# Woven rows: the order in device memory of the keys and values of a decode step on one core

## The chip, the cores and the metric

The kernel runs on one core of one Trainium2 chip. The metric is device microseconds (us) from launch to end. Three executions of the kernel before took 1299.92, 1299.98 and 1300.0 us; their median is 1299.98 us. The profile is of one more execution, of 1300.05 us, whose span from the first to the last instruction is 1298.7 us.

## The reference

One new token for each of two sequences (B = 2) attends to a cache of 32,768 positions. There are 32 query heads of 128 elements, and 8 heads of keys and values; each group of four query heads shares one of them. A small dense branch with a squared ReLU gates the result. Everything is float32.

```python
xn = layernorm(x)                                   # (2, 1, 512)
q = xn @ wq                                         # 32 heads of 128
scores = einsum("bhqd,bhkd->bhqk", q, k) * 128**-0.5
o = einsum("bhqk,bhkd->bhqd", softmax(scores), v)   # k, v: (2, 8, 32768, 128), each used by 4 heads
s = o.reshape(2, 1, 4096) @ wo
h = relu(xn @ w1 + b1); g = silu((h * h) @ w2 + b2)
out = x + s * g
```

Keys and values are 2 x 8 x 32768 x 128 x 4 bytes each, 268 MB, and each element is used once, for four heads. That is 537 of the 561 MB that the kernel reads.

## The kernel before, in words

**Tiles.** The 16 pairs of a sequence and a head of keys are taken one after the other, each in two halves of 16,384 positions: 32 half heads. For each there is one tile of keys and one of values. A tile is 128 partitions of 16,384 float32, that is 128 rows of 64 KiB, 8 MiB in all. For keys a partition is one of the 128 elements of a head, and its row runs over the positions; for values a partition is one position of each 128, and its row holds 128 positions with their 128 elements.

**Buffers.** There is one buffer for keys (kslot), one for values (vslot) and one for weights (wbuf), each of 64 KiB in every partition. A tile is not held twice: the next tile of keys may be fetched when the scores of the present one have been computed, and the next tile of values when the sums over the present one are done.

**Order of the work.** TensorE (PE) computes the scores of half head i from kslot (L351, 32 products of 512 columns, the queries being the stationary side), then the transposes that the softmax needs (L354, L357, L359), then the sums over the values from vslot (L368), then turns the result (L378). VectorE (DVE) and ScalarE (ACT) do the maximum, the exponential and the merging of the two halves. All of it runs in loops over the 32 half heads, written by hand with semaphores, one loop for each engine.

**The queue of fetches.** SyncE (SP) issues nearly all transfers, in the order of the program: first the weights of the dense branch (wm, into vslot) and wq (into wbuf), then the first tile of keys (L121). When the prologue has used vslot, the first tile of values follows (L231). Then, for each half head, SP waits for the scores (L240) and issues the next tile of keys (L241), waits for the sums over the values (L242) and issues the next tile of values (L244). The last tile of values comes in two halves by columns (L246, L247). After that follow the pieces of the output weights wo (L330). Each transfer is one instruction. The 16 DMA engines carry out a transfer together, each a share of its rows, and each takes up the next transfer in the queue when it is done with its share of the last.

**Rows in device memory.** In the host arrays `kt` and `vt` the row of partition p is row p of its tile, and after each row of 64 KiB lies a gap of GAP = 256 unused floats (1 KiB), put there by `gapped`. A fetch names 128 rows with a step of 16,640 floats at the source and 128 partitions at the destination. The weights wm, wq and wo lie without gaps.

Of the kernel before, what the change touches and what calls it, by code (L numbers as in the profile page):

```python
# [14 lines left out]
P = 128  # L15
B, D, HQ, HKV, SK, DH, F = 2, 512, 32, 8, 32768, 128, 1792
REP = HQ // HKV
NS = B * HKV
ND = D // P
NG = 4  # L20
# [4 lines left out]
SLOT = HALF  # L25
# [7 lines left out]
TAIL = (2, 1, 1)  # L33
NX = PIECES[0]
LINE = 256
GAP = 256
SCALE = 1.0 / math.sqrt(DH)


# [18 lines left out]
def build(nc, xr, x16, kt, vt, wq, wm, wo, out):  # L58
# [4 lines left out]

    def sb(name, *shape):
        return nc.alloc_sbuf_tensor(name, [P, *shape], F32)

    nc.sbuf_base = -(-nc.sbuf_base // LINE) * LINE
    kslot, vslot, wbuf = sb("kslot", SLOT), sb("vslot", SLOT), sb("wbuf", SLOT)
    prob, pT, o_sb = sb("prob", W), sb("pT", W), sb("o_sb", W)
    oS, oX, oN = sb("oS", NS, REP), sb("oX", NX, 16), sb("oN", TOP, M)  # L70
    ident = sb("ident", P)
    xb, gate, yb, gpad = sb("xb", P), sb("gate", P), sb("yb", P), sb("gpad", P)
# [11 lines left out]
    gv, ge, gb, gc, gd, gs, dm, ex, os, vh = (nc.alloc_semaphore(n) for n in ("gv", "ge", "gb", "gc", "gd", "gs", "dm", "ex", "os", "vh"))  # L84
# [17 lines left out]
    g, v = nc.gpsimd, nc.vector  # L102
# [15 lines left out]
    t_pad = pool.done(g.memset(vslot[:, WM:], 0.0))  # L118
    sp.wait(t_pad)
    nc.sync.dma_start(wbuf[:, :], wq).then_inc(wq_sem, 16)  # L120
    nc.sync.dma_start(kslot[:, :], kt[0, 0, :, 0:SLOT]).then_inc(gs, 16)  # L121
    nc.regs_mov(ss, 1)
    sp_hint = nc.sync.mark_branch_hint_location()
    v.memset(o_ps[:, :], 0.0).then_inc(dm, PRO)
# [49 lines left out]
    def pro(n, i):  # L174
        return pe.sem, 2 * i + n
# [52 lines left out]
    dve.wait(t_qz, t_q)  # L228
    v.tensor_copy(qz[:, 28:32], qT[:, 0, :]).then_inc(gs, 1)
    sp.wait(pro(VD, 2))  # L230
    nc.sync.dma_start(vslot[:, :], vt[0, 0, :, 0:SLOT]).then_inc(gv, 16)  # L231

    SD, MT, PT, LS, VD, OT = range(1, 7)

    def at(n, i):
        return pe.sem, 2 * PRO + 6 * i + n

    for i in range(NT - 1):
        s, u = divmod(i + 1, 2)
        sp.wait(at(SD, i))  # L240
        nc.sync.dma_start(kslot[:, :], kt[s, u, :, 0:SLOT]).then_inc(gs, 16)  # L241
        sp.wait(at(VD, i))  # L242
        if i + 2 < NT:
            nc.sync.dma_start(vslot[:, :], vt[s, u, :, 0:SLOT]).then_inc(gv, 16)  # L244
        else:
            nc.sync.dma_start(vslot[:, 0:SLOT // 2], vt[s, u, :, 0:SLOT // 2]).then_inc(gv, 16)  # L246
            nc.sync.dma_start(vslot[:, SLOT // 2:], vt[s, u, :, SLOT // 2:SLOT]).then_inc(gb, 16)  # L247
    nc.br("sp_last", engines=SP)

    dve.wait(t_selm, t_qT)  # L250
# [193 lines left out]
def packed(A_x, A_k_cache, A_v_cache, A_wq, A_wo, B_w1, B_b1, B_w2, B_b2):  # L444

    def c(a):
        return np.ascontiguousarray(a)

    def gapped(a):
        rows = np.zeros((NS, 2, P, SLOT + GAP), np.float32)  # L450
        rows[..., :SLOT] = a
        return rows

    x = np.asarray(A_x).reshape(B, D)
    k = np.asarray(A_k_cache).transpose(1, 0, 3, 2).reshape(NS, DH, 2, HALF).transpose(0, 2, 1, 3)
    v = np.asarray(A_v_cache).transpose(1, 0, 2, 3).reshape(NS, 2, NG, NJ, 4, P, DH).transpose(0, 1, 5, 4, 2, 3, 6).reshape(NS, 2, P, SLOT)
    wq = np.asarray(A_wq).reshape(ND, P, HQ * DH).transpose(1, 0, 2).reshape(P, SLOT)
    w1 = np.asarray(B_w1).reshape(ND, P, NF, P)
    w2 = np.asarray(B_w2).reshape(NF, P, D)
    wm = np.zeros((28, 4, P, P), np.float32)  # L460
    for d in range(ND):
        wm[4 * d:4 * d + 3] = w1[d][:, :12].reshape(P, 3, 4, P).transpose(1, 2, 0, 3)
        wm[3 + 4 * (d // 2), 2 * (d % 2):2 * (d % 2) + 2] = w1[d][:, 12:].transpose(1, 0, 2)
    wm[[11, 15] + list(range(16, 28))] = w2.reshape(NF, P, 4, P).transpose(0, 2, 1, 3)
    wm = np.concatenate([wm.transpose(2, 0, 1, 3).reshape(P, WM), np.zeros((P, SLOT - WM), np.float32)], axis=1)
    w = np.asarray(A_wo).reshape(HQ, DH, D)
    parts, h = [], 0
    for n in PIECES + TAIL:
        parts.append(w[h:h + n].transpose(1, 0, 2).reshape(n * P, D))
        h += n  # L470
    xr = np.zeros((8, D), np.float32)
    xr[:B] = x
    xr[B:6].reshape(-1)[:F] = np.asarray(B_b1)
    xr[6] = np.asarray(B_b2)
    return {"xr": c(xr.reshape(8, 2, D // 2).transpose(1, 0, 2)), "x16": c(x.reshape(B, NG, P).transpose(1, 0, 2).reshape(NG * B, P)), "kt": gapped(k), "vt": gapped(v), "wq": c(wq),
            "wm": c(wm), "wo": c(np.concatenate(parts))}


# [13 lines left out]
```

## Time and profile before

| | |
|---|---|
| median of three executions | 1299.98 us (1299.92 to 1300.0) |
| profiled execution, its span | 1300.05 us, 1298.7 us |
| PE busy | 689.8 us, 53% of the span |
| ACT, DVE busy | 99.1 us, 85.8 us |
| DMA queue of SP | 10,800 packets, 561.06 MB, 99.8% of 16 engines' span |
| read from device memory | 561.01 MB, 432 GB/s over the span |
| mean granted TensorE clock | 0.752 |

The page of the profile groups instructions by line, engine and tile, with the idle time of the engine before them and what ended it. A row of the chain of waits says when a piece of the work that ended last began, how long it lasted, and what it was; a transfer there is counted from its issue to its landing, with the time in the queue. A window gives, for a stretch of time, the busy time of each engine, the share of the DMA engines' time in which they moved packets, and the rate.

### The profile page before, as it was taken

To read this page: it belongs to the slowest core of one execution; us is meant where nothing else is said; L and a number is where in the kernel's file an instruction comes from. 1 tells how busy PE (TensorE), PEld (TensorE's weight loads), DVE (VectorE), ACT (ScalarE), POOL (GpSimd) and SP (SyncE) were. 2 spreads that over 40 slices of the span, in tenths; PEclk is the share of its full clock that TensorE was granted. 3 is DMA by queue.
4 is the path that set the end of the run, shared out by engine and by line. 5 is a ranking of instruction groups with operands and counts; after the bars stand their busy time and mean duration, and the time that the engine had idled before them with its cause. 6 is when DMAs were issued, how large, how long until landed. Compare 5 with 4: busy or idle time off the path is not lost.

```text
span 1298.7 us, 11201 instructions
## 1 busy us (share of the span) xinstructions
PE 689.8 (53%) x4781; PEld 191.1 (15%) x4781; DVE 85.8 (7%) x366; ACT 99.1 (8%) x202; POOL 5.7 (0%) x22
## 2 busy tenths in 40 slices
PE   3646546545645545544545644554654654554557
PEld 0111111111111111111111111111111111111112
DVE  2100000000000000000000000000000000000001
ACT  0301000010010001001000000001001000100100
POOL 1000000000000000000000000000000000000000
PEclk9877677778678777768777767767767777876878
DMA  9999999999999999999999999999999999999998
GB/s 420 420 452 420 446 426 420 452 420 452 420 452 420 442 430 420 452 420 452 420 452 420 442 430 420 452 420 452 420 452 420 444 428 424 448 420 452 420 436 373
DMA packets 10840, 561.08 MB, mean 432 GB/s; under 512 B 1216, under 2 KB 1368, under 8 KB 1752
## 3 DMA queue, kind: packets, MB, share of 16 engines
q1 hardware_dynamic: 10800, 561.06, 99.8%
q10 hardware_dynamic: 40, 0.02, 0.0%
HBM read 561.01 MB, written 0.07 MB: 432 GB/s over the span
## 4 chain that ended last, share of the span: by engine, by line
DMA 74%; PE 24%; issue 1%; DVE 0%; POOL 0%; SPq 0%; POOLq 0%
DMA vslot<-in_vt 70%; PE o_ps L368 24%; DMA wbuf<-in_wo 3%; DMA vslot<-in_wm 1%; PE wb L396 0%; DVE vslot L210 0%; PE acc L426 0%; PE acc L430 0%; POOL pT L201 0%; POOL pT L183 0%; SPq L247 0%; DVE pT L208 0%; SPq L246 0%; DVE yb L434 0%; DVE xb L436 0%
## 5 line engine op out<-in xcount | busy, mean ns | idle before, releaser
L368 PE MATMUL o_ps<-vslot,pT 128*16 128x512 f32 x2304 | 324.5, 726 | 223.1 <-DMA vslot<-in_vt 199.4
L351 PE MATMUL sc<-kslot,qz 128*32 128x512 f32 x2048 | 294.0, 739 | 279.2 <-DMA kslot<-in_kt 279.2
L351 PEld LDWEIGHTS sc<-kslot,qz 128*32 128x32 f32 x2048 | 71.3, 132 | 480.4 <-DMA kslot<-in_kt 286.8
L368 PEld LDWEIGHTS o_ps<-vslot,pT 128*16 128x16 f32 x2304 | 69.2, 112 | 449.2 <-issue 220.9
L313 ACT ACTIVATE prob<-sc,nm 128x512 f32<-128x512 f32 x32 | 22.0, 687 | 635.8 <-DVE nm L281 635.8
L274 DVE TENSOR_REDUCE r<-sc 128x1 f32<-128x512 f32 x32 | 22.1, 692 | 559.7 <-PE sc L351 559.7
L322 ACT COPY o_sb<-o_ps 128x512 f32<-128x512 f32 x32 | 18.7, 585 | 476.9 <-PE o_ps L368 476.9
L357 PE MATMUL tp<-ident,prob 128*128 128x128 f32 x128 | 26.9, 346 | 50.6 <-ACT prob L313 50.6
L295 DVE TENSOR_REDUCE t<-ot 128x4 f32<-128x64 f32 x32 | 7.2, 224 | 544.7 <-PE ot L378 544.7
L378 PE MATMUL ot<-ident,o_sb 128*128 128x128 f32 x140 | 23.0, 287 | 25.1 <-ACT o_sb L322 22.9
L357 PEld LDWEIGHTS tp<-ident,prob 128*128 128x128 f32 x128 | 17.2, 171 | 56.7 <-ACT prob L313 56.7
L354 PE MATMUL ms<-ident,r 128*128 128x128 f32 x32 | 10.3, 323 | 26.4 <-DVE r L274 26.4
L378 PEld LDWEIGHTS ot<-ident,o_sb 128*128 128x128 f32 x140 | 14.7, 141 | 57.3 <-ACT o_sb L322 52.4
L315 ACT COPY pT<-tp 128x512 f32<-128x512 f32 x32 | 18.7, 585 | 29.8 <-PE tp L357 29.8
L313 ACT ACT_TABLE_LOAD x16 | 20.5, 1283 | 0.3
L359 PEld LDWEIGHTS ms<-selh,l 128*128 128x128 f32 x64 | 12.9, 249 | 0.0
L354 PEld LDWEIGHTS ms<-ident,r 128*128 128x128 f32 x32 | 4.3, 133 | 55.4 <-DVE r L274 55.4
L359 PE MATMUL ms<-selh,l 128*128 128x4 f32 x64 | 10.9, 241 | 0.0
L277 DVE TENSOR_REDUCE mh<-ms 128x4 f32<-128x128 f32 x32 | 9.3, 291 | 10.9 <-PE ms L354 10.9
L204 ACT COPY vslot<-wbuf 128x4096 f32<-128x4096 f32 x2 | 7.1, 3605 | 0.2 <-DMA wbuf<-in_wq 0.2
L313 ACT ACTIVATION_READ_ACCUMULATOR prob<-sc,nm 128x1 f32 x32 | 6.2, 193 | 0.0
L396 PE MATMUL wb<-wbuf,oX 128*16 128x512 f32 x24 | 4.5, 906 | 2.2 <-DMA wbuf<-in_wo 2.2
(86 smaller groups left out, 78.1 us busy)
## 6 DMA issues: line engine op xcount, KB each, us to landing
vslot<-in_vt SPq DMA_DIRECT2D x2, 4096.0 KB, 23.9
vslot<-in_wm SPq DMA_DIRECT2D x1, 7168.0 KB, 19.4
wbuf<-in_wo SPq DMA_DIRECT2D x1, 3072.0 KB, 34.8
vslot<-in_wo SPq DMA_DIRECT2D x1, 2048.0 KB, 13.5
vslot<-in_wo SPq DMA_DIRECT2D x2, 1024.0 KB, 11.9
kslot<-in_kt SPq DMA_DIRECT2D x32, 29.4
wbuf<-in_wo SPq DMA_DIRECT2D x1, 512.0 KB, 13.8
wbuf<-in_wo SPq DMA_DIRECT2D x2, 256.0 KB, 14.0
```

The lines of the kernel that those rows point to most:

```text
L274: v.tensor_reduce(r1[:, :], sc[:, :], axis=AX.X, op=ALU.max).then_inc(dm, 1)
L277: did(f"mh{u}", v.tensor_reduce(mh[:, u, :], ms[:, :P].rearrange("p (a h) -> p h a", h=REP), axis=AX.X, op=ALU.max))
L295: did(f"t4{u}", v.tensor_reduce(t4[:, u, :], ot[:, :].rearrange("p (i y e) -> p e i y", i=4, y=NG)[:, :REP], axis=AX.XY, op=ALU.add))
L313: nc.scalar.activation(prob[:, :], sc[:, :], AF.Exp, bias=nm[:, u:u + 1], scale=SCALE, accum_out=l1[:, :]).then_inc(ex, 1)
L315: copy(pT[:, :], tp[:, :]).then_inc(gv, 1)
L322: copy(o_sb[:, :], o_ps[:, :]).then_inc(os, 1)
L351: ins = mm(sc[32 * c:32 * c + 32, :], qz[:, 28 - 4 * j:60 - 4 * j], kslot[:, lo:lo + W], start=(j == 0), stop=(j == NJ - 1))
L354: tr(ms[:, :P], r1[:, :].to_broadcast([P, P]), ident[:, :]).then_inc(pe.sem, 1)
L357: ins = tr(tp[:, k * P:(k + 1) * P], prob[:, k * P:(k + 1) * P], ident[:, :])
L359: mm(ms[:, :REP], l1[:, :].to_broadcast([P, P]), selh[:, :], start=True, stop=True).then_inc(pe.sem, 1)
L368: ins = mm(o_ps[32 * y:32 * y + 16, :], pT[:, 16 * n:16 * n + 16], vslot[:, n * W:(n + 1) * W], start=(n < NG), stop=(n >= 32 - NG))
L378: ins = tr(ot[:, lo:lo + P], o_sb[:, n * DH:(n + 1) * DH], ident[:, :])
```

## The change

Three things change together, for the tiles of keys and values alone.

- **No gap.** The rows of a tile lie one behind the other, 64 KiB each, and a tile is one block of 8 MiB.
- **The order of the rows.** `woven` puts the row of partition 8e + j at place 16j + e of the tile (e from 0 to 15, j from 0 to 7). So the rows of partitions 0, 8, 16, ... 120 come first, in one stretch of 1 MiB, then those of 1, 9, ... 121, and so on.
- **The form of the fetch.** The new helper `fetch` names the source as 16 times 8 rows: the outer dimension (e, 16 long) has a step of one row, the inner one (j, 8 long) a step of 16 rows. The destination is the same 128 partitions as before, in their order. All six places that fetch keys or values go through it, the two halves of the last tile of values too.

The program has the same instructions in the same order on every engine; the tiles hold the same numbers in the same places as before. The weights are fetched as before.

```diff
-GAP = 256
+NE = 16
...
+    def fetch(dst, src, sem):
+        nc.sync.dma_start(dst, src.rearrange("(j e) c -> e j c", e=NE)).then_inc(sem, 16)
...
-    nc.sync.dma_start(kslot[:, :], kt[0, 0, :, 0:SLOT]).then_inc(gs, 16)
+    fetch(kslot[:, :], kt[0, 0], gs)
...
-    nc.sync.dma_start(vslot[:, :], vt[0, 0, :, 0:SLOT]).then_inc(gv, 16)
+    fetch(vslot[:, :], vt[0, 0], gv)
...
         sp.wait(at(SD, i))
-        nc.sync.dma_start(kslot[:, :], kt[s, u, :, 0:SLOT]).then_inc(gs, 16)
+        fetch(kslot[:, :], kt[s, u], gs)
         sp.wait(at(VD, i))
         if i + 2 < NT:
-            nc.sync.dma_start(vslot[:, :], vt[s, u, :, 0:SLOT]).then_inc(gv, 16)
+            fetch(vslot[:, :], vt[s, u], gv)
         else:
-            nc.sync.dma_start(vslot[:, 0:SLOT // 2], vt[s, u, :, 0:SLOT // 2]).then_inc(gv, 16)
-            nc.sync.dma_start(vslot[:, SLOT // 2:], vt[s, u, :, SLOT // 2:SLOT]).then_inc(gb, 16)
+            fetch(vslot[:, 0:SLOT // 2], vt[s, u][:, 0:SLOT // 2], gv)
+            fetch(vslot[:, SLOT // 2:], vt[s, u][:, SLOT // 2:], gb)
...
-    def gapped(a):
-        rows = np.zeros((NS, 2, P, SLOT + GAP), np.float32)
-        rows[..., :SLOT] = a
-        return rows
+    def woven(a):
+        return np.ascontiguousarray(a.reshape(NS, 2, NE, P // NE, SLOT).transpose(0, 1, 3, 2, 4)).reshape(NS, 2, P, SLOT)
...
-"kt": gapped(k), "vt": gapped(v), "wq": c(wq),
+"kt": woven(k), "vt": woven(v), "wq": c(wq),
```

More of the change, by code (lines that the diff above doesn't have):

```diff
@@ L474, in packed @@
     xr[6] = np.asarray(B_b2)
-    return {"xr": c(xr.reshape(8, 2, D // 2).transpose(1, 0, 2)), "x16": c(x.reshape(B, NG, P).transpose(1, 0, 2).reshape(NG * B, P)), "kt": gapped(k), "vt": gapped(v), "wq": c(wq),
+    return {"xr": c(xr.reshape(8, 2, D // 2).transpose(1, 0, 2)), "x16": c(x.reshape(B, NG, P).transpose(1, 0, 2).reshape(NG * B, P)), "kt": woven(k), "vt": woven(v), "wq": c(wq),
             "wm": c(wm), "wo": c(np.concatenate(parts))}
```

## The prediction

> **What bounds the kernel now.** I read the page first: the DMA rows, the chain of waits, then the two groups in which TensorE does most of its work.
>
> ```profile
> span 1298.7 us, 11201 instructions
> ...
> DMA packets 10840, 561.08 MB, mean 432 GB/s; under 512 B 1216, under 2 KB 1368, under 8 KB 1752
> q1 hardware_dynamic: 10800, 561.06, 99.8%
> ...
> DMA 74%; PE 24%; issue 1%; DVE 0%; POOL 0%; SPq 0%; POOLq 0%
> ...
> L368 PE MATMUL o_ps<-vslot,pT 128*16 128x512 f32 x2304 | 324.5, 726 | 223.1 <-DMA vslot<-in_vt 199.4
> L351 PE MATMUL sc<-kslot,qz 128*32 128x512 f32 x2048 | 294.0, 739 | 279.2 <-DMA kslot<-in_kt 279.2
> ```
>
> The 16 DMA engines move packets for 99.8% of the span, and both large groups of TensorE sit idle for transfers (279.2 and 199.4 us). The 24% of PE in the chain are therefore not a second bound: they stand ahead of an issue, while the queue still works on the other buffer's tile. The chain in order of time (start, length, what) shows the cadence:
>
> ```profile
> 50.36 27.74 DMA vslot<-in_vt
> 78.10 0.04 issue
> 78.14 9.07 PE o_ps L368 x64
> ...
> 281.14 29.02 DMA vslot<-in_vt
> ...
> 319.31 29.44 DMA vslot<-in_vt
> ...
> 1207.36 30.11 DMA vslot<-in_vt
> ...
> 1248.60 34.82 DMA wbuf<-in_wo
> ```
>
> The first tile of values has landed at 78.10, the 31st at 1207.36 + 30.11 = 1237.47. Between them lie 30 tiles of values and 30 of keys: 1159.37 / 60 = **19.32 us a tile**. A tile is 128 rows of 65,536 bytes, so each of 16 engines moves 8 rows, 2.415 us a row, 27.1 GB/s an engine and 434 GB/s in all. All 64 tiles take 64 x 19.32 = 1236 us of the 1298.7; the rest is weights and the two ends.
>
> **What the rate does not depend on.** Three windows: the start of wm, the whole of wq, and the middle of the kernel (the last two columns are the DMA engines' busy share and GB/s).
>
> ```profile
> 1.70:4.50 2.80, 0.00 (x0) 0.00 (x0) 0.89 (x5) 1.28 (x1) 2.80 (x12) 1.00 1.10 369
> 19.40:38.70 19.30, 16.72 (x132) 4.10 (x132) 0.89 (x6) 0.58 (x1) 0.52 (x1) 1.00 1.00 431
> 600.00:1200.00 600.00, 321.21 (x2164) 89.29 (x2168) 34.97 (x157) 41.46 (x94) 0.00 (x0) 0.73 1.00 433
> ```
>
> wq is a tile of the same shape without gaps, and it moves at 431 GB/s, the gapped tiles at 433. Only the first packets of all, just after the launch, are slower (369). Next, three windows of 3 us in 40 slices of 75 ns, in which a packet's bytes stand where it starts: around the first row of keys (38 to 41 us), then 600 to 603 and 1200 to 1203.
>
> ```profile
> GB/s 0 0 0 0 0 0 0 0 874 1748 3495 1748 1748 2622 1748 0 0 0 0 0 0 0 0 0 0 0 0 0 0 0 0 0 0 0 0 0 0 0 0 0
> ```
>
> ```profile
> GB/s 0 0 0 0 0 0 0 0 0 0 0 0 0 0 0 0 0 0 0 0 0 3495 4369 874 874 1748 2621 0 0 0 0 0 0 0 0 0 0 0 0 0
> ```
>
> ```profile
> GB/s 0 0 0 0 0 0 3495 4369 874 874 1748 1748 874 0 0 0 0 0 0 0 0 0 0 0 0 0 0 0 0 0 0 0 0 0 0 0 0 0 2621 4369
> ```
>
> In each, the 16 engines start a row within 6 or 7 slices, some 0.5 us, and then none starts for 1.8 us or more. They are as closely in step after 1200 us as at 39. No engine falls behind, wherever its rows lie. I read from this that what sets 2.415 us a row is fixed in width, one to an engine, and lies behind the reading of device memory: in the engine itself, or where it writes.
>
> **The change part by part.** *No gap, and the rows woven at the source.* This touches the reading, which by the rows above does not set the pace. The bound on a gain: the two landings at 281.14 + 29.02 = 310.16 and 319.31 + 29.44 = 348.75 are 38.59 apart, the shortest two tiles I found, against 38.64 on the mean. Were all 32 pairs as short, 32 x 0.05 = 1.6 us would go, 0.12%. I take 0. The bound on a loss: the 369 GB/s of the first packets throughout, 1236 x (433/369 - 1) = +214 us; wq speaks for the other end, and I take 0 here too.
>
> *The issue of a fetch.* The program has the same 65 fetches. Their instruction has one more dimension. The issue times (least, median, most, in ns) of keys, and the slowest issue in the trace, that of a small input from ACT:
>
> ```profile
> L241 SPq DMA_DIRECT2D kslot<-in_kt x31: 327/328/328, 67.3 to 1227.3; - x31
> DMA to landing us min/median/max: 28.4/29.4/53.3
> ```
>
> ```profile
> L132 ACTq DMA_DIRECT2D xb<-in_x x1: 647/647/647, 2.1 to 2.1; - x1
> ```
>
> From 0.33 us to at most 0.65 is 0.32 more, 65 x 0.32 = 21 us if nothing hid it. It is hidden: a tile lands 29.4 us after its issue and takes 19.32, so it waits 10.1 us behind the other buffer's tile; if tiles get longer, this cover grows. I take 0.
>
> *Which partitions an engine writes.* The source now has an outer dimension of 16 where it had 128 rows. With 16 engines, the natural share of engine e is index e: 8 rows at the source, and at the destination the 8 neighbouring partitions 8e to 8e + 7, in that order. Every large transfer in the trace has 128 rows on both sides, so none shows such a split, nor does the trace tell which partitions an engine writes now. Two ends: if each engine still has what it writes into to itself, a tile stays at 19.32 us and the term is 0. If under the new split the engines meet two by two at one of the places that an engine has had to itself until now, with the others left idle, each gets half: 4.83 us a row, 38.64 us a tile, and 64 x 19.32 = **+1236 us**. Of the two I take the upper end. The rows point to a private path of fixed width as the limit, and the split at the destination is the one thing in this change that can take the privacy away.
>
> [...]
>
> Do the pairs stay in step? The spread of 0.5 us at the first row of keys is at most 0.2 of a row. [...] A tile has landed when its slowest pair has, so the pair closest in step decides, and I take 1.98, +1211 us.
>
> **The sum.** The span of 1298.7, and 1300.05 - 1298.7 = 1.35 around it: 1300.05 + 1211 + 0 + 0 = 2511 us; the profiled execution stands 0.07 us from the median of 1299.98. The queue does not run dry: keys are issued 9 us after their tile has landed (9.07 above for the values' products), while 38 us of the other tile are still to come. The stall goes to TensorE, which waits some 38 us more for each pair of tiles; nothing else is late. I say **2511 us**, 2410 to 2600 for this case (the lower end by 0.4 row of distance within pairs, 1300 + 0.9 x 1236; the upper if a tile takes 2.5% more than twice its time, 39.6 us).
>
> **The rivals.**
>
> *It changes nothing (1300 us, 1298 to 1302).* The split at the destination may be as good as the old one: because the limit sits in the engine and not where it writes, or because the hardware deals out the partitions as before whatever the source says. For it: rows take the same time for every tensor, and an engine of fixed width would look exactly like this. Against it: nothing in the trace, only that the form of the fetch is new. It decides if one row of keys still takes 2.415 us. This is the end on the other side.
>
> [...]
>
> *The sources collide (1300 + 214 = 1514 us).* Sixteen reads 64 KiB apart in step could keep meeting in one part of device memory, as perhaps the first packets do (369 GB/s). Against it: wq, without gaps, at 431.
>
> *Faster.* It would take more than the 1.6 us bounded above.
>
> **How the numbers follow.** In step 0.60, slipping apart 0.15, nothing 0.20, sources 0.03, faster 0.02. About 0.2%, 2.6 us, is what a measurement of this kernel can tell from no change. Slower is 0.60 + 0.15 + 0.03 = 0.78, the same 0.20, faster 0.02. Leaving out the case of no change would leave out more than 2 in 10, so the range reaches from it to the top of the likeliest: 1298 to 2600. It is wide because it holds two outcomes with little between; the likeliest alone is 2410 to 2600.
>
> **What would show it.** Right: the median time to landing of keys goes from 29.4 to about 38.3 - 9.1 + 38.3 = 67 us, the landings of values come some 76 us apart, a window in the middle shows about 219 GB/s with a DMA share still near 1.00, since each packet takes twice as long and no engine rests, and the idle time ahead of L351 grows by some 600 us. Wrong in its mechanism, though slow: a share near 0.5 at the same packet length (fewer engines at work), more packets of a smaller size (rows cut up), or a rate that climbs in the course of the kernel (pairs slipping apart). Wrong altogether: 433 GB/s and 38.6 us between landings, as before.

## The result, and the profile after

The changed kernel takes 2654.11 us (median of six executions, 2649.69 to 2655.28); the kernel before took 1299.93 us beside it. The ratio is 2.041, with a 95% interval of 2.039 to 2.0431. The predicted time was 2511 us and the range 1298 to 2600. The direction was as forecast, and so was the place of the loss, the destination (205 GB/s at partitions 0 to 63 against 413 at 32 to 95, below); the loss, 1354 us, was larger than the 1211 that were predicted.

The page of the changed kernel, at the places that were shown of before:

```profile
span 2653.3 us, 11201 instructions
...
DMA packets 10840, 561.08 MB, mean 211 GB/s; under 512 B 1216, under 2 KB 1368, under 8 KB 1752
...
q1 hardware_dynamic: 10800, 561.06, 100.0%
...
another core or an unknown queue 69%; PE 25%; DVE 2%; DMA 2%; issue 1%; ACT 1%; POOL 0%; SPq 0%; POOLq 0%; DVEq 0%
...
L371 PE MATMUL o_ps<-vslot,pT 128*16 128x512 f32 x2304 | 326.4, 729 | 900.9 <-DMA vslot<-in_vt 877.0
L354 PE MATMUL sc<-kslot,qz 128*32 128x512 f32 x2048 | 294.4, 740 | 956.0 <-DMA kslot<-in_kt 956.0
```

There are as many packets and as many bytes as before, and the engines rest no more than before (100.0% of 16 engines' span). They move half as much in the same time: 211 GB/s instead of 432. TensorE works as long as before (294.4 us against 294.0 in the scores), and its idle time ahead of the scores has grown by 677 us. The chain of waits no longer names the transfers: a transfer now lands 72 us after its issue, and the view puts such a wait down to an unknown queue. The groups still name them.

The windows, with the start (wq, fetched as before) first, then the middle; the last two columns are the DMA share and GB/s:

```profile
19.40:38.70 19.30, 16.39 (x132) 4.05 (x132) 0.89 (x6) 0.98 (x2) 0.89 (x2) 1.00 1.00 431
...
600.00:1200.00 600.00, 151.25 (x1041) 41.20 (x1041) 16.41 (x75) 20.24 (x44) 0.00 (x0) 0.62 1.01 208
```

wq, in the old form, still moves at 431 GB/s. The slow rate begins with the first fetch of the new form. The issues of keys and values, from SP's instructions in order of time (start, length), and the issues of the keys' tile with the times to landing:

```profile
89.59 0.54 SPq L68 DMA_DIRECT2D kslot<-in_kt  x1
130.32 0.54 SPq L68 DMA_DIRECT2D vslot<-in_vt  x1
...
2519.77 0.54 SPq L68 DMA_DIRECT2D kslot<-in_kt  x1
```

```profile
L68 SPq DMA_DIRECT2D kslot<-in_kt x32: 536/537/654, 5.4 to 2519.8; - x32
...
DMA to landing us min/median/max: 70.9/71.7/74.7
```

From the second issue of keys to the last there are 30 pairs of tiles: (2519.77 - 89.59) / 60 = **40.50 us a tile**, against 19.32 before. 64 x (40.50 - 19.32) = 1356 us, which is the whole loss. In the packet records of the trace the rows of keys and values come in fours: one of 4.92 us, then three of 5.12.

### The profile page after: what moved, and what is told of

It is laid out like the page before. It is cut to its first block, busy times and chain, and to the rows that moved or that the text cites. A ratio compares the mean times of both kernels' runs of the same rounds, so it can differ in the third digit from the quotient of the medians.

```text
span 2653.3 us, 11201 instructions
## 1 busy us (share of the span) xinstructions
PE 690.6 (26%) x4781; PEld 190.7 (7%) x4781; DVE 86.1 (3%) x366; ACT 99.1 (4%) x202; POOL 5.7 (0%) x22
## 4 chain that ended last, share of the span: by engine, by line
another core or an unknown queue 69%; PE 25%; DVE 2%; DMA 2%; issue 1%; ACT 1%; POOL 0%; SPq 0%; POOLq 0%; DVEq 0%
PE o_ps L371 11%; PE sc L354 11%; DMA wbuf<-in_wq 1%; PE tp L360 1%; DVE r L277 1%; PE ot L381 1%; ACT o_sb L325 1%; DMA wbuf<-in_wo 0%; PE ms L357 0%; DVE mh L280 0%; ACT prob L316 0%; DVE mm L282 0%; DVE nm L284 0%; PE ms L362 0%
## 5 line engine op out<-in xcount | busy, mean ns | idle before, releaser
L354 PE MATMUL sc<-kslot,qz 128*32 128x512 f32 x2048 | 294.4, 740 | 956.0 <-DMA kslot<-in_kt 956.0
L320 ACT COPY lh<-ms 128x4 f32<-128x4 f32 x32 | 5.4, 168 | 0.0
## 6 DMA issues: line engine op xcount, KB each, us to landing
vslot<-in_wm SPq DMA_DIRECT2D x1, 7168.0 KB, 19.3
kslot<-in_kt SPq DMA_DIRECT2D x32, 71.7
```

What stands on the lines that cost most here:

```text
L354: ins = mm(sc[32 * c:32 * c + 32, :], qz[:, 28 - 4 * j:60 - 4 * j], kslot[:, lo:lo + W], start=(j == 0), stop=(j == NJ - 1))
```

## The experiments

Two theories were at odds with each other, and each could still have taken part. *Where it writes*: by the form of the new fetch an engine writes 8 neighbouring partitions, and the engines meet two by two at places that take one engine's rate. *What it reads, or how it is asked to*: rows without gaps side by side collide when they are read in step, or the longer form of the fetch is slower by itself. And for the size: is the time above twice the old (40.5 instead of 38.6 us) part of the meeting, or something added by the reading? The trace does not name the engine of a packet: which engine writes which partitions, and how many meet at a place, is inferred from the form of the fetch, here and in the expectations. That four neighbouring partitions are one place, and that partitions 32 apart in one half share one, is supposed there and tested by rates alone. The rates and the lengths of the rows are measured.

**No gap, old form.** The kernel before with one number changed.

```diff
-GAP = 256
+GAP = 0
```

> The kernel before with GAP = 0: the rows of a tile lie one behind the other, and the fetch names 128 rows as before. It does one part of the change alone, the missing gap. If the place of the writing decides (the engines meet where they write), the gap is innocent: 1300 us, within 0.2%. [...]

It took 1299.91 us; the ratio is 1.0001, interval 0.9991 to 1.0011. Its window from 600 to 1200 us:

```profile
600.00:1200.00 600.00, 318.49 (x2164) 87.94 (x2168) 35.02 (x157) 41.46 (x94) 0.00 (x0) 0.74 1.00 433
```

The missing gap is innocent, and by itself it brings nothing either.

**New form, rows in the order of the partitions, with gaps.** Nothing is woven here; only the split is that of the change. A ninth row, unused, follows every eight, so that the source keeps its two steps.

```diff
+GAP = 256
...
-        nc.sync.dma_start(dst, src.rearrange("(j e) c -> e j c", e=NE)).then_inc(sem, 16)
+        nc.sync.dma_start(dst, src).then_inc(sem, 16)
...
-    fetch(kslot[:, :], kt[0, 0], gs)
+    fetch(kslot[:, :], kt[0, 0, :, 0:8, 0:SLOT], gs)
...
+        rows = np.zeros((NS, 2, NE, P // NE + 1, SLOT + GAP), np.float32)
+        rows[:, :, :, :P // NE, :SLOT] = a.reshape(NS, 2, NE, P // NE, SLOT)
...
```

> The new form of the fetch (16 times 8 rows) over rows that lie in the order of the partitions, each with its gap of 1 KiB: nothing is woven, no rows lie side by side without a gap. It undoes the source's part of the change and keeps the split. If the place of the writing decides: as the changed kernel, 2654 us within 1%, and the 4.8% above twice the time of a tile (40.5 us instead of 38.6) are there too, since they belong to the sharing. If reading woven rows decides: 1300 us. If the sharing costs exactly half and the woven reading the 4.8% on top: 1300 + 64 x 19.32 = 2536 us less the distance within pairs, so 2510 to 2536.

It took 2652.69 us, a ratio of 2.0405 (2.0365 to 2.0446), and the window reads as that of the changed kernel:

```profile
600.00:1200.00 600.00, 152.76 (x1041) 42.38 (x1041) 16.41 (x75) 20.24 (x44) 0.00 (x0) 0.61 1.00 206
```

So the order of the rows in device memory has no part that shows in the loss, nor in the excess over twice the time. Left are the form and the destination.

**The same fetch at two destinations.** After the first tile of keys, both kernels fetch 64 rows a tile in the new form, from the same woven rows. They differ in one number, the partition at which the 64 rows begin: BASE is 0 in the one shown and 32 in the other.

```diff
+BASE, ROWS = 0, 64
...
-        nc.sync.dma_start(dst, src.rearrange("(j e) c -> e j c", e=NE)).then_inc(sem, 16)
+        nc.sync.dma_start(dst[BASE:BASE + ROWS], src[0:ROWS].rearrange("(j e) c -> e j c", e=NE)).then_inc(sem, 16)
```

> The changed kernel, but after the first tile of keys each fetch brings only 64 rows into partitions 0 to 63 (the other partitions keep what stood there, so half of the keys and values are left out). Each engine gets 4 neighbouring partitions: engine e partitions 4e to 4e+3. If places 32 partitions apart are shared, engines e and e+8 meet all the time: 5.12 us a row, 20.3 us a half tile, 206 GB/s at a DMA share of 1.00, the whole 19 + 63 x 20.3 + 64 = 1360 us. If what counts is the form or the woven source alone: the same as the next run.

> As the run at partition 0 in every word of the fetch, but the 64 rows go to partitions 32 to 95 (the others keep what stood there). Engine e writes partitions 32+4e to 35+4e; if partitions p and p+32 of one half of 64 share a place, no two engines meet. Then a row takes 2.42 us, 27.1 GB/s an engine: rate over DMA share 433 GB/s, a half tile 9.7 us, and TensorE with some 24 us a half head becomes the bound: 800 to 900 us in all. If the form of the fetch or the woven source slows the engines: 206 GB/s at a share of 1.00 and 1360 us, as at partition 0.

At partition 0 it took 1372.8 us, at partition 32 780.13. The windows, first at 0, then at 32:

```profile
300.00:1200.00 900.00, 420.61 (x3058) 114.35 (x3058) 48.97 (x220) 59.57 (x132) 0.00 (x0) 0.75 1.00 205
```

```profile
300.00:700.00 400.00, 320.56 (x2530) 97.15 (x2526) 40.25 (x181) 49.33 (x109) 0.00 (x0) 0.91 0.92 380
```

205 GB/s at a share of 1.00 against 380 / 0.92 = 413. In the packet records the rows at 0 take 5.12 us, the fourth like the first, and the median row at 32 takes 2.42. (Some rows at 32 are longer, up to 4.03 us, mostly where the engines start again after a rest; hence 413 and not 433.) The form, the source and the number of bytes are the same, so the destination alone makes the difference. (At 32 the transfers no longer bound all of it: the chain of waits goes to TensorE for 50% of the span and to transfers for 40%.) This is the experiment that settles what sets the rate. That engine e writes the partitions from 4e on at 0 (from 32 + 4e at 32), and which of them meet, is inferred from the form; that it matters which 64 partitions are written is measured.

**16 and 32 rows at partition 0.** The kernel at partition 0 with `BASE, ROWS = 0, 16` and `0, 32`.

> After the first tile of keys each fetch brings only 16 rows into partitions 0 to 15, one to an engine (seven eighths of the keys and values are left out). Four engines then write four neighbouring partitions. If four neighbours share one place, a row takes four times as long: 9.66 us if sharing itself costs nothing, 10.24 us and 102 GB/s at a DMA share of 1.00 if it costs the 5.9% that two show (5.12 against 4.83), whatever their number; more than 10.4 us and under 101 GB/s if the cost grows with the number. If only places 32 partitions apart were shared, 433 GB/s. TensorE or the chain of a half head becomes the bound, some 24 us each, 800 us in all; the rate is read over the DMA share.

> The same with 32 rows into partitions 0 to 31, two to an engine (three quarters of the keys and values are left out): engines 2i and 2i+1 write the same four neighbouring partitions, and none of them is 32 partitions from another's. If four neighbours share a place: 5.12 us a row, 206 GB/s over the DMA share, as with engines 32 partitions apart, so that the cost of sharing is the same for both ways of meeting. If only the distance of 32 makes them meet: 2.42 us a row and 433 GB/s.

They took 769.54 and 779.41 us. Their windows, 16 rows first:

```profile
200.00:700.00 500.00, 411.31 (x3207) 126.64 (x3211) 50.87 (x230) 63.19 (x142) 0.00 (x0) 0.89 0.84 97
```

```profile
200.00:700.00 500.00, 404.12 (x3137) 121.50 (x3141) 49.92 (x226) 61.59 (x137) 0.00 (x0) 0.89 0.92 191
```

With 32 rows, 191 / 0.92 = 208 GB/s, and 5.12 us at the median row of the packet records: the price of the 64 rows at 0 (205 GB/s, 5.12 us). So at the same rate of 205 to 208, partitions 32 to 63 add nothing to what 0 to 31 take. By the form of the fetch, two engines write the same four neighbours here, and there two write 32 partitions apart. With 16 rows, 97 / 0.84 = 115 GB/s, more than the 102 that I had expected from the price of two. The engines start and stop here, which blurs the rate; in the packet records the rows range from 7.1 to 9.64 us. The tiles come in pairs without a pause between them. In the second of a pair, where I take four engines to be at work at a place from a row's beginning to its end, the rows gather at 9.60 to 9.64 us (136 of the 928 rows after 100 us, none longer). If four share a place there, that is 4 x 65,536 bytes in 9.64 us, **27.2 GB/s** for the place: 9.64 us is less than four times 2.418 (9.67), so the excess of the two is not there.

**Keys in pieces, old form, all the work done.** The kernel before, each tile of keys in fetches of 16, or of 64, partitions in their order, with the gaps. The one by 16 is shown; in the other, 64 stands for 16 and `i * 33 + 1` for `i * 129 + 1`.

```diff
+    def pieces(dst, src, sem):
+        for p in range(0, P, 16):
+            nc.sync.dma_start(dst[p:p + 16], src[p:p + 16]).then_inc(sem, 16)
...
-        nc.sync.dma_start(kslot[:, :], kt[s, u, :, 0:SLOT]).then_inc(gs, 16)
+        pieces(kslot, kt[s, u, :, 0:SLOT], gs)
...
-        w(gs, i * 17 + 1)
+        w(gs, i * 129 + 1)
```

> The kernel before, but each tile of keys comes in eight fetches of 16 partitions in their order, one row for each engine, old form, gaps kept. All the work is done. Four engines share a place, for all of a tile. If sharing costs nothing more than the division: 4 x 2.415 = 9.66 us a row, 77.3 us a tile of keys, 1300 + 32 x 58.0 = 3155 us. If each sharing costs 5.9%, as for two: 10.23 us, 81.8 us a tile, 3300 us. If the cost grows with the number: above 3350 us.

> The kernel before, but each tile of keys comes in two fetches of 64 partitions, old form of the source (64 rows one after the other), gaps kept. All the work is done. Partitions 0 to 63 hold only half of the places, so two engines share each. If the price belongs to two engines at one place, however the fetch is written: 5.12 us a row, 41 us a tile of keys, 1300 + 32 x 21.6 = 1992 us, 1970 to 2000. If the 5.9% belong to the new form or the woven rows: 38.6 us a tile and 1918 us. If only the new form makes engines meet: 1300 us.

By 64 it took 1994.63 us (ratio 1.5345, interval 1.5314 to 1.5375), as expected for two at one place (5.12 us a row), though the form of the source is the old one. By 16, two executions took 3111.41 and 3223.99 us; the profile is of the longer one. A tile of keys in each, the windows reaching from its first row to the first row of the next tile, 16 first:

```profile
132.70:206.00 73.30, 9.28 (x68) 2.27 (x68) 0.23 (x1) 0.59 (x1) 0.00 (x0) 0.57 1.00 114
```

```profile
98.50:138.70 40.20, 10.47 (x68) 2.45 (x68) 0.23 (x1) 0.59 (x1) 0.00 (x0) 0.58 1.01 209
```

By 64, two at one place by the form of the fetch, it is 40.2 us a tile, more than twice 19.32 (38.6). By 16, four at one place, it is 73.3 us, less than four times 19.32 (77.3), but I do not take this for the rate of one place. In the packet records the 16 engines begin the second row of this tile up to 1.7 us apart, and 32 rows at partition 0 moved 208 GB/s where 16 moved 115. From these I infer that an engine that is ahead already writes at the next place while the others are still at the last; no run shows it. For four at one place I go by the run with 16 rows, 9.64 us a row. Neither run shows a tax on every sharing: the excess is there with two (40.2 us against 38.6), and not with four (9.64 us a row against 9.67). Three were not tried.

The expectation of 3155 us for no excess lies between the two times, but not for its reason. With 73.3 us a tile it would be 1300 + 32 x 54.0 = 3028 us. The profiled execution took 196 us more, and most of that is not accounted for. In its later part the values' rows take about 2.75 us instead of 2.42, which adds some 33 us to an engine's time over the whole profile, and single rows among them take 3 to 5 us (packet records). From 2000 to 3000 us the rate is 166 GB/s at a share of 0.95, which is 101 us for a pair of tiles instead of 73.3 + 19.3.

**The change for the keys alone**, with the values in the old form, without their gap and with it; the one without is shown, the other fetches `vt[s, u, :, 0:SLOT]`.

```diff
-            fetch(vslot[:, :], vt[s, u], gv)
+            nc.sync.dma_start(vslot[:, :], vt[s, u]).then_inc(gv, 16)
...
-"kt": woven(k), "vt": woven(v), "wq": c(wq),
+"kt": woven(k), "vt": c(v), "wq": c(wq),
```

> The change for the keys alone; the values are fetched as 128 rows without gap. If each tile is priced by its own split, 32 tiles of keys at 40.5 us and 32 of values at 19.3: 1300 + 32 x 21.16 = 1977 us, 1965 to 1990. If the fetches of keys leave the engines out of step for the values or the other way round: under 1950 us.

> The change for the keys alone as before, but the values keep their gap of 1 KiB. In the run without that gap the values' rows took 2.418 us in some tiles and 2.714 us in others, the same for all 128 rows of a tile. If the missing gap is the cause (rows read in step collide at the source): all tiles of values at 2.418 us, 1977 to 1985 us, with a spread of a few us between executions. If it comes from the change of the split between two tiles: again tiles at 2.714 us, and times from 1980 to 2040 us.

Without the gap, the profiled execution took 1998.87 us, and another 2029.35. Two stretches of it, one in the first tile of values and one in the fourth:

```profile
80.00:99.00 19.00, 9.61 (x71) 2.94 (x71) 1.38 (x5) 1.43 (x4) 0.00 (x0) 0.77 1.00 386
267.00:284.00 17.00, 9.99 (x71) 3.01 (x71) 2.29 (x11) 1.54 (x5) 0.00 (x0) 0.80 1.00 432
```

In the packet records, 25 of the 32 tiles of values take 2.418 us a row and 7 take 2.714. 7 x 8 x 0.296 = 17 us, so 1982 without them: the sum of the two prices holds to 0.3%. With the gap, the median row of every tile of values of the profiled execution takes 2.418 us and it took 1986.93 us, but the four executions scatter: 1986.93, 1987.69, 2026.33 and 2133.55 us. That is neither what the first theory expected (a spread of a few us) nor, in the one that was profiled, the second. In the run by 16 above, the values have their gap, and their rows slow down all the same. So a missing gap is not needed for it. What slows the values' rows between the slow tiles of keys is open; the whole-kernel change does not show it, since there no tile of keys or values is in the old form.

## Why the prediction was right or wrong

- **The bound** was read rightly: in these runs the reading does not set the rate of a row. Without the gap it is 433 GB/s as with it, woven or not woven 206 to 208; and one and the same reading goes at 205 to partitions 0 to 63 and at 413 to 32 to 95.
- **No gap and weaving, 0 us**: right (1.0001, and 2652.69 against 2654.11).
- **The issue**: bounded by 0.65 us, measured 0.54 against 0.33, 65 x 0.21 = 14 us. They are hidden, as said: the cover grew from 10.1 us to 71.7 - 40.5 = 31.2.
- **Which partitions an engine writes**: the upper end was taken, and the rates halved. The pair of kernels at partitions 0 and 32 shows that the destination decides; that engines meet there two by two is inferred. The doubt in the prediction, that the hardware may deal out the partitions as before whatever the source says, is settled by the runs together. Over the same 128 partitions the new form moves 206 GB/s with the rows not woven, and the old form 433; at partitions 32 to 95 the new form moves 413. So the form is not slow by itself; what is left, by inference, is that it changes which engine writes where at a time.
- **The step that failed is the size of that term**: "each gets half: 4.83 us a row, 38.64 us a tile, +1236 us". Measured are 5.12 us a row, 6% more than twice 2.415. 64 x 8 x (5.12 - 4.83) = +148 us, against a difference of 2654 - 2511 = 143 between the times. The prediction took the rate of one engine for the capacity of a place, and supposed that it is shared without loss. The first holds as far as the runs go (27.2 GB/s for a place in the run with 16 rows, if four share it); the second fails for two. Nothing in the trace of before could tell, since there the rows take about 2.42 us throughout; my allowance of 2.5% on a tile was too small (40.50 us is 4.8% above twice 19.32), and with it the upper end of 2600. The runs show the excess for four fetches: the new form with 128 rows, with 64 and with 32 rows at partition 0 (5.12 us at the median row of each), and the old form by 64 (40.2 us a tile). With 16 rows at partition 0 it does not show (9.64 us a row). What it is made of stays open.
- **The pairs in step**: the factor of 1.98 instead of 2, a deduction of 25 us, was my estimate, and no run shows it as such, nor the 0.9 in the lower end of the range. What the changed kernel shows in its place is that the first row of every four takes 4.92 us instead of 5.12, 128 x 0.20 = 26 us, and at 2500 us just as at 60. In the half tiles at partition 0, four rows to an engine, the first row takes 5.12 as well.
- **Slipping apart**, a rate that climbs in the course of the kernel, does not show in the changed kernel: from 80 to 600 us the rate is 206 GB/s, from 1800 to 2400 us it is 208, about the same.

```profile
80.00:600.00 520.00, 133.72 (x905) 37.31 (x905) 14.75 (x65) 17.67 (x40) 0.00 (x0) 0.61 1.00 206
...
1800.00:2400.00 600.00, 151.97 (x1041) 41.27 (x1041) 15.52 (x69) 20.13 (x43) 0.00 (x0) 0.61 1.01 208
```

- **What would show it**: share at 1.00 with the rate halved, as many packets, landing times of 71.7 (67 said), and 677 us more idle time ahead of the scores (600 said). Each is off by what the size of the one term is off.

## What to carry to other kernels

When a fetch is rewritten, look at both ends of it. Here a new outer dimension at the source, with the same 128 partitions at the destination, took a row from 2.42 us to 5.12, and in that form 64 rows took 5.12 us each at partitions 0 to 63 and 2.42 at 32 to 95. That it changes which partitions each DMA engine writes, so that engines meet, is inferred. DMA engines busy for 100.0% of the span at half the rate, with as many packets as before, went with it here; the busy share alone does not tell it from the kernel before (99.8%), and no run here shows how slow reading would look. Where the profile shows one rate for every source layout, expect little of a new one: here it is 433 GB/s with the gap and without, 1299.91 us against 1299.98. The cheapest test of a suspected destination is the same fetch at another first partition.

## What was not expected of the hardware

- Two engines at one place, if the form of the fetch is read rightly, move 2 x 65,536 bytes in 5.12 us, 25.6 GB/s, less than one alone (27.1). Four, in the run with 16 rows, move 4 x 65,536 in 9.64 us, 27.2 GB/s, and two stay 6% below that. So the loss shows with two and not with four, and why is open.
- In the runs with the change for the keys alone, old-form fetches of values take 2.714 us a row in some tiles and 2.418 in others, nearly all rows of a tile alike, and with the values' gap the executions scatter by 7% (1986.93 to 2133.55 us). The cause was not found.
